# Fourier mixing and tanh shrink on one core: first-stage steps in the third gap alone, output stores issued ahead of the next transposes, other queues and warm-up passes before the main loop

## The chip, the core and the metric

The kernel runs on one core of a Trainium2 chip. The metric is the time of one execution on the device in microseconds (us), as the median of several runs. TensorE is called PE, VectorE DVE, ScalarE ACT, GpSimd POOL and SyncE SP, as in the profile. Everything is computed in float32.

## The reference

```python
X = np.fft.rfft(x, axis=1)                 # x: (8, 3008, 256)
F = (filt_r + 1j * filt_i)[None, :, :]     # (1505, 256) each
y = np.fft.irfft(X * F, n=x.shape[1], axis=1).astype(np.float32)
t = y.reshape(8 * 3008, 256)
h = t @ moe_w_in                           # (256, 2048)
g = h - np.tanh(h)
out = (g @ moe_w_out).astype(np.float32)   # (2048, 256)
```

The two weights come in as float64 and are converted on the chip.

## The kernel before, in words

**The transforms.** The sequence of 3008 is split into 64 times 47. A batch element passes through three stages. The *first* stage (`first`, six steps of a batch) multiplies blocks of x with a matrix f over the 64 and stores the result in the DRAM tensor `ct1`. The *middle* stage (`middle`, seven slots of up to five frequencies, 58 steps of a batch) goes over the 47 forwards (products pa and pb), multiplies with the filter on DVE, goes back (product pe) and stores in `ct2` through a tile e. The *last* stage (`last`, once for each group) makes the tokens of a group: it loads a tile e2 (called e in the profile, too) and a matrix gt, multiplies them (product pu), and forms ut from an ACT copy and two DVE operations. A batch has six groups, so there are 48 groups in all.

**The main loop.** For each group and each quarter u of the 2048 hidden columns there is one unit U, 192 in all. A unit runs the products of w_in (`up`, tiles x, y, z), the shrink function (`shrink`: three activations of 1024 elements for each half, then a DVE product h) of the unit before, and the products of w_out (`down`, tiles o) of the unit before that. Seven products stand for eight through sums of blocks (Strassen's way), which POOL forms (`combine`, tiles t and tu). For the first four units (`up_plain`, `down_plain`) there are eight plain products.

**The order is written out by hand.** What a unit does stands in program order in `up`: x and y products; gap t(0); two down products; gap t(1); x, z; two down products; gap t(2); x; two down products; x; gap t(3); one down product; gap t(4); z. (For groups 0, 6, 12 and so on, t(1) and t(3) stand a little elsewhere.) These five places are the first to the fifth gap. In each gap `t(k)` issues, in this order: the stores of a first-stage step made earlier (list `written`, on ACT), in the third gap the DVE transposes of a finished output tile (`store`, tile ot, which has one buffer), four of the waiting output stores (`store_some`, on SP, 32 or 48 for a group), and one step of the first or middle stage that is due. The list `steps` holds the steps of a batch with their due places, sorted; of the first two, the first that is due and allowed is taken. The third gap of every fourth quarter is kept for `last`. From the fourth unit on a first-stage step may stand in the second and third gap of the first three quarters, unless a step pb stood in the gap before.

**Banks.** A step of the first stage (for batches from 3 on, in quarter form: 64 by 64 tiles of the array, 16 instructions) needs two PSUM banks, tags t and y. The bank y also holds the y product of the unit, until DVE has added it (L549). A middle step takes t, or y in some of the second to fourth gaps.

**Within a unit on ACT**: a copy s of x behind the first x product, a copy u behind each of the next two x products, and between them the activations of `shrink`. The next x product accumulates in the same bank and waits for the copy. A quarter step adds an ACT copy (L285) and two DVE operations (L286, L287), a back step pe an ACT copy (L379) and a store from ACT's queue (L381).

**DMA semaphores.** All DMAs from SP and ACT together take turns on eight completion semaphores, in program order, and those from POOL on eight others. A DMA waits, on the engine that issues it, until the one that had its semaphore before has landed.

**The prologue** handles batch 0 as a whole and part of batch 1 with its own tiles (`first0`, `across`, `back0`), converts the first weights (`early`, then `late`), and loads the tile e of group 0 piece by piece (`rest`, L981: eight loads; 25 rows each of slots 0 to 4, then 7 rows each of slots 5 and 6). Slots 0 to 4 are stored to `ct2` from POOL, slot 5 from ACT, slot 6 half from ACT and half from SP (L381). `warmer(n)` issues n products whose result is not used.

Of the kernel before, what the change touches and what calls it, by code (L numbers as in the profile page):

```python
# [21 lines left out]
SG = 5  # L22
# [4 lines left out]
NC = NH // CH  # L27
NX = NH // XH
SLOTS = [(a, min(SG, NA - a)) for a in range(0, NA, SG)]
KM = SG * NH  # L30
# [67 lines left out]
def kernel(  # L98
# [114 lines left out]
    def begun(tiles, job, queue=nc.sync):  # L213
        j = converted(tiles, *job, queue)
        next(j)
        return j
# [583 lines left out]
    def store_some(n):  # L800
        for dst, src in outs[:n]:
            nc.sync.dma_start(dst, src)  # L802
        del outs[:n]
# [93 lines left out]
    with tc.tile_pool(name="tr", bufs=2) as tr, tc.manual_schedule():  # L897
# [12 lines left out]
        with tc.tile_pool(name="pro", bufs=1) as pro, \  # L910
# [26 lines left out]
            def warmer(n, t=None):  # L937

                warm = z0("warm", [128, 256])
                t = f0[:, 0:2].rearrange("p a n -> p (a n)") if t is None else t  # L940
                for _ in range(n):
                    nc.tensor.matmul(warm, t[:, 0:128], t, start=True, stop=True)
# [34 lines left out]
            def rest(a, n, queues):  # L977

                e2 = e2s[0][0]
                for j in range(4):  # L980
                    queues[j % len(queues)].dma_start(  # L981
                        e2[NA * j + a:NA * j + a + n],
                        dram(ct2[0], (NA * j + a) * NH * DM, [[NH * DM, n], [1, CH * DM]]))

            def back0(g, nn):

                way = ways(g, 1, KM)
                for v in range(2):
                    pe = z0("pe", [128, 2, DM])[0:KM]
                    for k in range(2):  # L990
                        nc.tensor.matmul(pe[:, k], way[2 * v + k], nn[:, k],
                                         start=True, stop=False)
                        nc.tensor.matmul(pe[:, k], way[3 - k if v else 0], nn[:, 2 + k],
                                         start=False, stop=True)
                    e1 = pro.tile([128, 2, DM], F32, tag="e1", bufs=4, name="e1")[0:KM]
                    ACT.copy(e1, pe)
                    (G if g < len(SLOTS) - 2 else ACT).dma_start(
                        next(parts(ct2, 0, g, v, 2, 2))[2], e1)

            pairs = []  # L1000
# [102 lines left out]
            def way_back():  # L1103

                product, what = ended.pop(0)
                for _ in product(*what) or ():
                    pass
# [4 lines left out]
            for g in range(last_g + 1):  # L1112
                if g + 2 <= last_g:
                    fts[g + 2] = filters_of(g + 2)
                    a2[g + 2] = across(g + 2)
                if g == 3:
                    e2s[0] = load_e2(0, 0, ())
                    ones_1 = first1(load_x(big([128, 8, DM], F32, "x1"), 1, 0, 8))
                if g == last_g - 1:
                    under(fts[last_g])  # L1120
                    convert(3)
                    way_back()
                if g < last_g:
                    there[g + 1] = there0(g + 1)
                next(there[g][0])
                if g < last_g - 1:
                    convert(3)
                xy = there.pop(g)[1]
                chain = filtered(g, xy, fts.pop(g), V, V if g >= last_g - 1 else G, pro)
                nn = next(chain)  # L1130
                for _ in range(2):
                    next(chain)
                if g in summed:
                    next(chain)
                ended.append((back, (0, g, xy, z0, (ACT, nc.sync))) if g in summed else (back0, (g, nn)))
                if g not in (0, last_g - 1):
                    way_back()
                if g == 1:
                    next(turning)
                if g == 2:  # L1140
                    ahead = [begun(tiles1, job, queue=G) for job in jobs[5:7]]
            way_back()
            rest(0, SG * (last_g - 1), [nc.sync])
            rest(SG * (last_g - 1), NA - SG * (last_g - 1), [nc.sync])
            fs = first(2, z2, [(1, c) for c in range(2, NX)])
            next(fs)
# [3 lines left out]
            next(late)  # L1150
            for _ in ones_1:
                pass
            warmer(10)

        with tc.tile_pool(name="dn", bufs=2) as dn, \
                tc.tile_pool(name="ps", bufs=1, space=bass.MemoryType.PSUM) as ps:
# [46 lines left out]
            total = 4 * len(groups)  # L1203
            for _ in last(0, z2):
                pass
            for _ in range(4):
                next(late)
            def planned(p):
# [12 lines left out]
            for U in range(total + 2):  # L1221
                i, u = divmod(U, 4)
                if U == 6:
                    assert not pending
                    late = sums(7)
                if U < total:
                    p, c = groups[i]
                    if c == 0 and u == 0:
                        steps = planned(p)
                    if u == 0 and i + 1 < len(groups) and c + 1 < NC:  # L1230
                        e2s[i + 1] = load_e2(*groups[i + 1])
                    if u == 2 and i + 1 < len(groups) and c + 1 == NC:
                        assert not steps
                        e2s[i + 1] = load_e2(*groups[i + 1])
                    if u == 1 and c + 1 == NC:
                        for gens, ahead, what in ((mids, 2, middle), (firsts, 3, first)):
                            if p + ahead < BATCH:
                                gens[p + ahead] = what(p + ahead, z1 if what is middle else z2)
                                next(gens[p + ahead])
                    if u == 2 and i + 1 < len(groups):  # L1240
                        lasts = last(i + 1, z2)
                sh = shrink(U - 1) if 0 <= U - 1 < total else iter(())
                dw = iter(())
                if 0 <= U - 2 < total:
                    dw = (down if U - 2 >= 4 else down_plain)(U - 2)

                def converting(n):

                    for _ in range(n):
                        if next(late, pending) is pending:  # L1250
                            pending.clear()

                def d():

                    next(dw, None)

                def e():

                    next(dw, None)
                    converting(3 if U > 1 else 1)  # L1260

                def s():

                    next(sh, None)

                def t(k):

                    now[:] = U, k
                    if k == 0 and U >= 4:
                        taken.clear()  # L1270
                    while written:
                        ACT.dma_start(*written.pop(0))
                    if k == 2 and stores:
                        store(*stores.pop())
                    store_some(4)
                    if U >= total:
                        return
                    pos = 20 * c + 5 * u + k
                    if i == 1 and pos == LEAD - 7:
                        mids[1] = middle(1, z1)  # L1280
                        next(mids[1])
                    if u == 3 and k == 2 and i + 1 < len(groups):
                        next(lasts)
                    else:
                        due = [s for s in steps[0:2] if s[0] <= pos and
                               (s[3] is middle or U < 4 or
                                u < 3 and 0 < k < 3 and taken.get("slow") != k - 1)]
                        if due:
                            steps.remove(due[0])
                            _, gens, b, what, n = due[0]  # L1290
                            if b not in gens:
                                gens[b] = what(b, z1 if what is middle else z2)
                                next(gens[b])
                            next(gens[b])
                    converting(2)
                    if k and U > 1:
                        next(copies, None)

                if U < total:
                    if U == total - 1:  # L1300
                        ones = cst.tile([128, 1], F32, name="ones")
                        G.memset(ones, 1.0)
                    (up if U >= 4 else up_plain)(U, d, e, s, t)
                else:
                    for k in range(5):
                        s()
                        s()
                        d()
                        if U == total + 1 and k in (0, 2):
                            next(bound)  # L1310
                        e()
                        t(k)
# [39 lines left out]
```

## Time and profile before

| | |
|---|---|
| median of three runs | 2680.51 us (2680.18 to 2681.63) |
| the profiled execution | 2680.11 us, its span 2678.3 us |
| PE busy | 2641.6 us, 99% of the span |
| DVE, ACT, POOL busy | 66%, 63%, 49% |
| mean granted clock of PE | 0.994 |
| DMA | 198.20 MB, 74 GB/s over the span |

The span goes from the first to the last instruction. A row of a timeline reads: start, duration (us), engine, line, operation, out<-in, shapes, number of instructions merged, and in brackets the idle time before it and what ended it. `ACTq` and `SPq` are the queues of ACT and SP, whose DMA issues are not counted as busy. A matrix product in float32 stands as two instructions, and the end of a product overlaps the start of the next, so the pace is read from start to start. The granted clock is 1.00 at full speed and 0.50 at half.

### The profile page before, as it was taken

What the parts mean: (1) busy time and instruction counts of PE and PEld (TensorE: products, weight loads), DVE (VectorE), ACT (ScalarE), POOL (GpSimd) and SP (SyncE); (2) the same over time, 40 slices, a digit from 0 to 9 for tenths busy, and PEclk for the clock granted to TensorE, in tenths of its full rate; (3) what the DMA queues carried; (4) which work ended last, traced back from release to release, by engine and by line L of the source; (5) the groups of instructions that cost most, each with busy time, mean ns of one, the idle gap of its engine ahead of it and who ended that gap; (6) DMA issues with size and microseconds to landing.
All of it is one profiled execution on the core that took longest, in us unless ns stands there. A gap on an engine that the chain in (4) does not pass through costs nothing.

```text
span 2678.3 us, 41269 instructions
## 1 busy us (share of the span) xinstructions
PE 2641.6 (99%) x15460; PEld 2292.6 (86%) x15460; DVE 1780.1 (66%) x2234; ACT 1684.2 (63%) x2517; POOL 1312.4 (49%) x1084
## 2 busy tenths in 40 slices
PE   8899999999999999999999999999999999999998
PEld 7578889888898888988889888898888988898887
DVE  6677766767576675767657776577666776655555
ACT  4465666666666666666666666666666666666665
POOL 4116455544454554555455545455455554555552
PEclk9899999999999999999999999999999999999999
DMA  8753332331334313432234232423322221111110
GB/s 221 229 157 87 80 71 69 92 86 39 72 75 104 72 37 74 101 76 68 53 70 105 65 73 53 99 66 75 73 56 57 51 66 42 29 28 26 22 24 18
DMA packets 341960, 198.20 MB, mean 74 GB/s; under 512 B 240415, under 2 KB 312715, under 8 KB 341687
## 3 DMA queue, kind: packets, MB, share of 16 engines
q1 hardware_dynamic: 300877, 137.21, 22.4%
q10 hardware_dynamic: 36698, 45.63, 6.0%
q0 software_dynamic: 4176, 12.64, 1.6%
q8 instruction: 123, 2.02, 0.3%
q14 instruction: 86, 0.70, 0.1%
HBM read 123.22 MB, written 75.00 MB: 74 GB/s over the span
## 4 chain that ended last, share of the span: by engine, by line
PE 91%; DMA 3%; DVE 2%; issue 1%; ACT 1%; SPq 1%; POOL 0%; ACTq 0%; DVEq 0%; POOLq 0%
PE o L696 40%; PE x L526 24%; PE z L526 12%; PE y L526 6%; PE pe L376 3%; PE pu L485 2%; PE pb L328 2%; PE pa L328 1%; PE pf L280 1%; PE o L750 1%; DMA out_dram<-ot 1%; DMA filt<-in_filt_r_dram 1%; SPq L802 0%; PE pf L268 0%; DMA ct<-a 0%
## 5 line engine op out<-in xcount | busy, mean ns | idle before, releaser
L696 PE MATMUL o<-t,wd 128*128 128x256 f32 (+1 forms) x3008 | 759.7, 375 | 0.0
L648 DVE TENSOR_TENSOR h<-h,y 128x1024 f32<-128x1024 f32 (+1 forms) x384 | 553.3, 1441 | 167.8 <-ACT y L644 167.3
L506 POOL TENSOR_TENSOR t<-h 128x512 f32<-128x512 f32 (+1 forms) x186 | 256.4, 1379 | 819.2 <-DVE h L648 763.6
L696 PEld LDWEIGHTS o<-t,wd 128*128 128x128 f32 x3008 | 570.5, 190 | 67.3
L526 PE MATMUL x<-tu,wu 128*128 128x256 f32 (+1 forms) x2256 | 580.5, 380 | 4.7 <-ACT u L532 4.6
L696 PE MATMUL o<-h,wd 128*128 128x256 f32 (+1 forms) x2256 | 570.0, 375 | 1.8 <-DVE h L648 1.8
L526 PEld LDWEIGHTS x<-tu,wu 128*128 128x128 f32 x2256 | 418.7, 190 | 73.8 <-issue 12.5
L696 PEld LDWEIGHTS o<-h,wd 128*128 128x128 f32 x2256 | 427.6, 190 | 52.5 <-DVE h L648 2.6
L532 ACT COPY s<-x 128x512 f32<-128x512 f32 (+1 forms) x188 | 108.7, 578 | 538.6 <-PE x L526 529.6
L638 ACT ACTIVATE y<-h 128x1024 f32<-128x1024 f32 (+1 forms) x384 | 400.3, 1042 | 16.5 <-ACT e L379 9.6
L641 ACT ACTIVATE y<-y 128x1024 f32<-128x1024 f32 (+1 forms) x384 | 399.3, 1040 | 12.1
L644 ACT ACTIVATE y<-y 128x1024 f32<-128x1024 f32 (+1 forms) x384 | 399.9, 1041 | 5.1 <-ACT a L270 0.4
L532 ACT COPY u<-x 128x512 f32<-128x512 f32 (+1 forms) x376 | 215.1, 572 | 100.5 <-PE x L526 76.6
L507 POOL TENSOR_TENSOR t<-h,t 128x512 f32<-128x512 f32 (+1 forms) x186 | 266.6, 1433 | 14.6
L509 POOL TENSOR_TENSOR t<-h,t 128x512 f32<-128x512 f32 (+1 forms) x186 | 264.3, 1421 | 0.0
L508 POOL TENSOR_TENSOR t<-h 128x512 f32<-128x512 f32 (+1 forms) x186 | 261.0, 1403 | 0.0
L574 DVE COPY h<-x 128x512 f32<-128x512 f32 (+1 forms) x188 | 127.9, 681 | 131.6 <-PE x L526 130.8
L566 DVE TENSOR_TENSOR h<-z,u 128x512 f32<-128x512 f32 (+1 forms) x188 | 126.8, 674 | 99.6 <-ACT u L532 98.3
L526 PE MATMUL x<-ut,wu 128*128 128x256 f32 (+1 forms) x752 | 190.3, 375 | 0.0
L526 PE MATMUL y<-ut,wu 128*128 128x256 f32 (+1 forms) x752 | 190.1, 375 | 0.0
L526 PE MATMUL z<-tu,wu 128*128 128x256 f32 (+1 forms) x752 | 190.0, 375 | 0.0
L526 PE MATMUL z<-ut,wu 128*128 128x256 f32 (+1 forms) x752 | 190.0, 375 | 0.0
(163 smaller groups left out, 2969.2 us busy)
## 6 DMA issues: line engine op xcount, KB each, us to landing
e<-ct SPq DMA_DIRECT2D x47, 512.0 KB
ct<-e ACTq DMA_DIRECT2D x86, 240.0 KB
a<-ct SPq DMA_DIRECT2D x42, 480.0 KB
ft<-filt SPq DMA_DIRECT2D x42, 480.0 KB
out_dram<-ot SPq DMA_DIRECT2D x1248, 16.0 KB
x_sb<-in_x_dram SPq DMA_DIRECT2D x74, 256.0 KB
ct<-a ACTq DMA_DIRECT2D x62, 256.0 KB
gt<-g SPq DMA_DIRECT2D x48, 128.0 KB
```

Of the source, the lines that this page charges most:

```text
L506: by.tensor_sub(t[0], b[0][1], b[0][0])
L507: by.tensor_sub(t[1], b[1][1], t[0])
L508: by.tensor_sub(t[2], b[1][1], b[0][1])
L509: by.tensor_sub(t[3], b[1][0], t[1])
L526: nc.tensor.matmul(bank[:, k], wu[:, q - 1, (2 * u + k) * 128:(2 * u + k + 1) * 128], rhs[q - 1], start=(first and k == 0), stop=True, ski ...
L532: ACT.copy(t, X)
L574: V.tensor_copy(h[:, 2, :, 0:w], X)
L638: ACT.activation(y[k], ht[k], AF.Arctan, scale=TURN)
L641: ACT.activation(y[k], y[k], AF.Tanh, scale=BEND)
L644: ACT.activation(y[k], y[k], AF.Square, scale=SCALE, accum_out=y_sums[:, 2 * U + k // 2:2 * U + k // 2 + 1])
L648: V.tensor_mul(ht[k], ht[k], y[k])
L696: nc.tensor.matmul(product(q), wd[:, q - 1, (2 * u + k) * 128: (2 * u + k + 1) * 128], rhs[q - 1][:, k], start=(u == 0 and k == 0 and q == ...
```

## The change

1. First-stage steps (from unit 4 on) stand in the third gap of the first three quarters alone, and the condition on pb is gone. In the built program five of the six steps of each batch from 3 on move from the second gap to the third, 25 in all; the sixth stood there already. Middle steps around them move by a gap.
2. In a gap the four output stores are issued ahead of the transposes of the next tile, not behind, so a tile's first four stores stand one gap later in the order.
3. The generators of the next `middle` and `first`, with their first loads on SP, are begun in the third quarter of a batch's last group instead of the second; `last` is made where it is used.
4. Slot 5's two stores are issued from POOL, not from ACT.
5. The four loads of rows of slots 0 to 4 are issued on SP ahead of slot 6's way back and its stores.
6. `warmer(14)` for `warmer(10)`, and four more warm-up products behind the products pu of group 0.

```diff
@@ -994,7 +994,7 @@
-                    (G if g < len(SLOTS) - 2 else ACT).dma_start(
+                    G.dma_start(
                         next(parts(ct2, 0, g, v, 2, 2))[2], e1)
@@ -1139,8 +1139,8 @@
+            rest(0, SG * (last_g - 1), [nc.sync])
             way_back()
-            rest(0, SG * (last_g - 1), [nc.sync])
             rest(SG * (last_g - 1), NA - SG * (last_g - 1), [nc.sync])
@@ -1150,7 +1150,7 @@
-            warmer(10)
+            warmer(14)
@@ -1203,6 +1203,9 @@
             for _ in last(0, z2):
                 pass
+            warm = psl([128, 256], "o3")
+            for _ in range(4):
+                nc.tensor.matmul(warm[0:KM], mats[:, 0:KM], mats[:, 0:256], start=True, stop=True)
@@ -1232,13 +1235,11 @@
-                    if u == 1 and c + 1 == NC:
+                    if u == 2 and c + 1 == NC:
                         for gens, ahead, what in ((mids, 2, middle), (firsts, 3, first)):
                             if p + ahead < BATCH:
                                 gens[p + ahead] = what(p + ahead, z1 if what is middle else z2)
                                 next(gens[p + ahead])
-                    if u == 2 and i + 1 < len(groups):
-                        lasts = last(i + 1, z2)
@@ -1270,21 +1271,20 @@
+                    store_some(4)
                     if k == 2 and stores:
                         store(*stores.pop())
-                    store_some(4)
                     if U >= total:
                         return
...
-                    if u == 3 and k == 2 and i + 1 < len(groups):
-                        next(lasts)
+                    if (u, k) == (3, 2) and i + 1 < len(groups):
+                        next(last(i + 1, z2))
                     else:
                         due = [s for s in steps[0:2] if s[0] <= pos and
-                               (s[3] is middle or U < 4 or
-                                u < 3 and 0 < k < 3 and taken.get("slow") != k - 1)]
+                               (s[3] is middle or U < 4 or u < 3 and k == 2)]
```

## The prediction

> **What bounds the kernel now.** I read the page first, then the busy times by stage, then the waits and the timelines of the places where TensorE (PE) stood still. The page, its first lines and the chain that ended last:
>
> ```profile
> span 2678.3 us, 41269 instructions
> PE 91%; DMA 3%; DVE 2%; issue 1%; ACT 1%; SPq 1%; POOL 0%; ACTq 0%; DVEq 0%; POOLq 0%
> ```
>
> The busy times by stage (stretch, its length, then busy time of PE, PEld, DVE, ACT, POOL, the granted PE clock, DMA share, GB/s):
>
> ```profile
> 0.00:200.00 200.00, 179.26 (x866) 133.09 (x866) 138.28 (x243) 102.89 (x165) 51.13 (x69) 0.94 0.72 203
> 200.00:2640.00 2440.00, 2433.90 (x14466) 2135.97 (x14465) 1622.76 (x1964) 1565.61 (x2330) 1254.76 (x1008) 1.00 0.27 64
> 67.97:85.02 17.05, 14.06 (x72) 11.78 (x71) 10.83 (x22) 5.58 (x11) 2.22 (x3) 1.00 0.70 209
> 85.03:95.26 10.23, 5.83 (x69) 3.87 (x70) 4.41 (x8) 1.15 (x2) 0.16 (x1) 0.50 0.89 242
> 129.41:136.22 6.81, 5.99 (x10) 3.26 (x11) 3.68 (x10) 0.76 (x2) 0.72 (x1) 0.50 0.38 115
> ```
>
> PE is the bound, and the change takes no real product away. What can be won is PE's idle time: 20.7 us before 200 us, 6.1 us in the 2440 us of the main loop, and the time that PE runs at half clock (10.23 us after one gap in the prologue, 6.81 us after another). The rest is product time.
>
> **The prologue: loads, queues, warm-up passes.** PE's rows around the start of the main loop, and the ACT and DVE rows between them:
>
> ```profile
> 78.10 4.48 PE L942 MATMUL warm<-f 128*128 128x256 f32 x20
> 87.49 2.49 PE L485 MATMUL pu<-gt,e 64*64 64x64 f32 x64 [4.91 <-DMA x_sb<-in_x_dram]
> 90.06 0.59 ACT L489 COPY odd<-pu 128x512 f32<-128x512 f32 x1 [8.99 <-issue]
> 91.89 3.35 PE L596 MATMUL x<-ut,wu 128*128 128x448 f32 x4 [1.91 <-DVE ut L493]
> 95.04 1.78 PE L596 MATMUL z<-ut,wu 128*128 128x448 f32 x4
> 101.39 1.67 PE L596 MATMUL x<-ut,wu 128*128 128x448 f32 x4
> 102.89 1.67 PE L596 MATMUL z<-ut,wu 128*128 128x448 f32 x4
> 130.24 1.86 PE L750 MATMUL o<-h,wd 128*128 128x448 f32 x2 [3.21 <-DVE wd L179]
> 200.27 1.16 PE L485 MATMUL pu<-gt,e 64*64 64x64 f32 x64
> ```
>
> After ten warm-up passes PE waits 4.91 us for the tile e of group 0 (the releaser is named x_sb, but pu reads only gt and e). Then the clock is 0.50 until 95.26: pu takes 2.49 us instead of 1.16, and the four x rows 3.15 us (91.89 to 95.04) instead of 1.50 (101.39 to 102.89). What holds the tile e, by queue:
>
> ```profile
> 67.14 0.74 POOL L997 DMA_DIRECT2D ct<-e  x1 [2.50 <-ACT e L996]
> 69.81 0.74 POOL L997 DMA_DIRECT2D ct<-e  x1 [1.93 <-ACT xy L331]
> 70.55 0.74 POOL L153 DMA_DIRECT2D raw<-in_moe_w_out_dram  x1
> 72.15 0.60 ACTq L997 DMA_DIRECT2D ct<-e  x1
> 73.83 0.34 ACTq L997 DMA_DIRECT2D ct<-e  x1
> 74.81 1.17 SPq L381 DMA_DIRECT2D ct<-e  x2
> 78.74 0.28 SPq L981 DMA_DIRECT2D e<-ct  x1
> 80.27 1.76 SPq L981 DMA_DIRECT2D e<-ct  x5
> ct<-e POOLq DMA_DIRECT2D x1, 240.0 KB, 3.0
> 74.81 5.14 DMA ct<-e
> ```
>
> The first four loads of e need only slots 0 to 4, whose last stores (POOL, 67.14 and 69.81) land 3.0 us after issue, at 72.8. But they stand behind the two SP stores of slot 6, and the second takes over the semaphore of slot 5's first ACT store (72.15), so it goes out only at 78.74, 6.6 us behind that store.
>
> Changed: (1) the four loads come ahead of the slot 6 stores and no longer follow an ACT store; they go out between 70.1 and about 74. (2) Slot 5's two stores go out on POOL ahead of the raw weight loads, at about 72.2 and 73.9, and by the 3.0 us row land by 77. POOL's two raw loads start 3 to 4 us later; nothing else stands behind them on POOL, and the conversions that use them come behind pu in the order of ACT and DVE. (3) The SP stores of slot 6 keep 74.81, since their copies set it. They land 3.0 us (the POOL row) to 5.1 us (the chain's row) later, at 78 to 80. (4) The last four loads then go out by 79.5 to 81. Before, the last was issued at about 81.7 and PE started 5.75 us later; 3.0 is the other end. So e is there between 82.5 and 86.8. I take 83.5, near the early end, because the four large loads no longer stand in front of them.
>
> (5) Fourteen passes at 0.448 us (4.48 for ten) end at 84.4 instead of 82.6, so pu starts at 84.4 with no gap to speak of and full clock. pu 1.16, the wait of 1.91 for ACT and DVE, then x at 87.5 and z at 89.0 against 95.04: **6.0 us**. The four new passes behind pu take 4 x 0.448 = 1.8 us inside the 1.91 us wait; without that cover they would cost up to 1.8. If e comes at 86.8, the gain is about 1. What lies behind is a chain of relative waits and should move along, and the second gap (3.21 us ahead of 130.24, with the half clock of 129.41) should stay. If it went too, another 3.2 us of idle and half of 6.8 us would go.
>
> [...]
>
> **The main loop: first-stage steps.** The waits of PE between 400 and 2640 us, all of them (engine, line, releaser: us, times, longest):
>
> ```profile
> PE x L526 <- ACT u L532: 4.4, 5, 0.9
> PE pf L280 <- DVE h L549: 1.4, 5, 0.5
> ```
>
> Five of each: once per batch. The second kind, with the DVE rows that cause it:
>
> ```profile
> 858.91 1.76 DVE L366 TENSOR_TENSOR xy<-nn 120x512 f32<-120x512 f32 x1
> 860.47 0.65 PE L280 MATMUL pf<-x_sb,f 64*64 64x256 f32 x4
> 862.34 1.13 PE L526 MATMUL x<-tu,wu 128*128 128x256 f32 x4
> ```
>
> A quarter step in the second gap needs both banks; y is freed by DVE's L549, here queued behind the adds of the step in the first gap (L366 until 860.67). It takes 1.87 us (860.47 to 862.34). Such a step in the third gap already stands in the trace once per batch:
>
> ```profile
> 625.09 1.09 PE L280 MATMUL pf<-x_sb,f 64*64 64x256 f32 x16
> 626.12 1.13 PE L526 MATMUL x<-tu,wu 128*128 128x256 f32 x4
> 627.08 1.89 PE L696 MATMUL o<-t,wd 128*128 128x256 f32 x8
> 627.28 0.59 ACT L532 COPY u<-x 128x512 f32<-128x512 f32 x1 [0.42 <-PE x L526]
> 628.81 1.03 PE L526 MATMUL x<-tu,wu 128*128 128x256 f32 x4
> ```
>
> It takes 1.03 us, and u is copied at 627.87, 0.94 us before PE needs it at 628.81. The change moves 25 steps (five per batch) from the second gap to the third. Five are worth 0.84 each, **4.2 us**; the other 20 cost and win nothing. The middle step that leaves the third gap goes to the second or fourth, where such steps stand already. For the bound above: the copy L285 now stands ahead of the u copy on ACT; if ACT comes an activation (1.06) later than at 627, 0.12 is lost per step, 3 us in all.
>
> **The main loop: stores.** The first kind of wait:
>
> ```profile
> 680.88 3.08 DMA out_dram<-ot
> 682.29 1.89 PE L696 MATMUL o<-t,wd 128*128 128x256 f32 x8
> 684.03 0.35 ACTq L381 DMA_DIRECT2D ct<-e  x1
> 685.06 1.13 PE L526 MATMUL x<-tu,wu 128*128 128x256 f32 x4 [0.88 <-ACT u L532]
> ```
>
> The store of e on ACT takes over the semaphore of the first output store behind the transposes (680.88), waits until it lands, and holds up the u copy behind it on ACT. The same eight products take 1.73 us at 627.08 (to 628.81), so 685.06 is 1.04 late; five times, **5.2 us**. In the changed order the first-stage step stands in this gap, its ct stores and the e store come a gap later, when the output stores ahead have been out longer, and the next u copy stands ahead of them. What is late then is the copy s of the next step: its use has the slack of a gap (0.9) or more. Ends: 0 won (the wait moves to s) and 5.2; I take 5.2, since the same layout at 625 us has no wait. The first loads of the two stages that run ahead start one unit later, two units before their use; a unit is about 13.4 us (192 of them between 91.89 and the tail), so 27 us are left for transfers of 3 to 6: nothing.
>
> **Sum.** 6.0 + 4.2 + 5.2 = 15.4 us off the profiled execution of 2680.11 (span 2678.3 and 1.8 around it): 2664.7. The runs' median is 0.4 above it: **2665**.
>
> **Rivals.** (B) The prologue's gain is given back, since e lands at 86.8 or DVE's weight conversions set the pace before 130 us anyway: 9.4 to 10.4 us are left, 2671. For it: DMA share 0.89 in that stretch; against: the chain is one of waits on each other. (C) The main loop's waits only move (the e store waits for a later output store, the step for the bank of the middle step ahead of it): 6.0 are left, 2674.5. For it: a group's output stores still go out in a row while ACT stores; against: 625 us. (D) Both, so that the change does not do what it says: 2680. (E) Slower: in the third gap ACT is regularly late, its copy L285 ahead of u, and PE waits at the second x product behind it. Price per step: two activations (2.12) less the 0.94 of slack = 1.18, times 25 = 29.5, so 2694. It decides from (15.4 + 5.4) / 25 = 0.83 us per step. Against it: no such wait in five steps of before; for it: a late u copy does reach PE (685.06).
>
> [...] The trace has 0.50 from 129.41, when the stop that ended at 130.24 was 2.4 us old, so a late e of two or three us would cost clock as well.
>
> **How the numbers follow.** Forecast 0.60 (own range 2660 to 2670: the moved copy up, a shorter second gap down), B 0.12, C 0.12, D 0.06, E 0.10. 0.2% is 5.4 us, about what a measurement can tell from no change. Faster 0.84, same 0.06, slower 0.10. The range takes in B and C, and below, the second gap gone: 2658 to 2676.
>
> **What would show it.** Right: PE's idle time before pu under 1 us, no 0.50 clock between 85 and 95 us, z at about 89; 30 quarter steps of 1.03 us behind the second down products, no PE wait on L549; no ACT store waiting ahead of a u copy once per batch. Wrong: waits of x on u or s in every batch, of y L526 on the copy L379, or a clock of 0.50 behind 85 us. The prediction falls if waits of over 0.8 us stand behind most moved steps.

## The result: 2670.7 us against 2680.4, and the profile after

| | before | after |
|---|---|---|
| median of six runs each, on the same chip | 2680.35 us (2680.11 to 2681.63) | 2670.68 us (2669.85 to 2671.94) |
| ratio, 95% interval | | 0.9961 [0.9951, 0.9972] |
| profiled execution: time, span | 2680.11, 2678.3 us | 2670.29, 2668.5 us |
| mean granted clock of PE | 0.994 | 0.997 |

The change makes the kernel 9.7 us faster. The forecast was 15.4 us faster: the right side, inside the range of 2658 to 2676, but 5.7 us short. The page of after, its first line and the chain that ended last:

```profile
span 2668.5 us, 41319 instructions
PE 94%; DVE 2%; DMA 2%; ACT 1%; issue 1%; SPq 0%; ACTq 0%; POOL 0%; DVEq 0%; POOLq 0%
```

The busy times by stage of after (columns as in the prediction):

```profile
0.00:200.00 200.00, 184.30 (x973) 138.74 (x974) 145.02 (x251) 104.98 (x169) 57.70 (x75) 0.98 0.71 202
84.20:91.00 6.80, 6.48 (x80) 4.23 (x81) 4.14 (x8) 1.69 (x3) 0.00 (x0) 1.00 1.04 259
124.30:127.70 3.40, 3.15 (x5) 1.52 (x6) 2.05 (x6) 0.22 (x2) 0.67 (x1) 0.50 0.50 190
213.05:219.85 6.80, 5.79 (x14) 4.57 (x15) 3.98 (x6) 1.63 (x3) 1.63 (x2) 0.50 0.39 122
```

The clock is full where it was 0.50 before (85 to 95 us), and the half-clock stretch at the second gap is 3.4 us long in place of 6.8. But there is a new one of 6.8 us from 213, in a place where before had none.

To see where the time went, cut both traces at points that they share and compare the lengths. The points are the first product L1079, the first z product L596, and the first pu product of groups 1, 2, 3, 4 and 47:

| stretch | before | after | difference |
|---|---|---|---|
| start to L1079 (PE has met no edit yet) | 74.65 | 73.22 | -1.43 |
| L1079 to z | 20.39 | 16.29 | -4.10 |
| z to group 1 | 45.34 | 43.77 | -1.57 |
| group 1 to 2 | 59.89 | 58.16 | -1.73 |
| group 2 to 3 | 56.04 | 64.53 | +8.49 |
| group 3 to 4 | 57.16 | 57.16 | 0.00 |
| group 4 to 47 | 2285.82 | 2275.04 | -10.78 |
| group 47 to the end | 79.05 | 80.35 | +1.30 |

The eight add up to -9.82 us, the difference of the spans. The first is put down to chance: L1079 came at 73.9 to 75.0 us in the profiles of the four programs with the old queues, and at 73.2 to 76.4 in the ten with the new. In the last, the way from the product L814 to the end is 1.3 us longer. That is hardly chance: it takes 11.8 to 12.4 us in all eight profiles of the changed kernel and of those made from it below, and 10.7 to 11.2 in the six of the kernel before and of those made from that. What causes it stays open. The -1.73 is a step of L268 (a row of x8) that moved from the stretch behind group 1 into the next, so the two stretches together have lost 6.8 us.

**The prologue.** PE's rows of after that answer to 78.10 to 95.04 and 130.24 of before:

```profile
76.67 6.21 PE L942 MATMUL warm<-f 128*128 128x256 f32 x28
84.19 0.33 PE L485 MATMUL pu<-gt,e 64*64 64x64 f32 x4 [1.31 <-DMA e<-ct]
84.84 1.15 PE L485 MATMUL pu<-gt,e 64*64 64x64 f32 x60 [0.32 <-issue]
85.92 1.99 PE L1208 MATMUL pt<-mats_sb 120*120 120x256 f32 x8
87.90 1.77 PE L596 MATMUL x<-ut,wu 128*128 128x448 f32 x4
89.50 1.67 PE L596 MATMUL z<-ut,wu 128*128 128x448 f32 x4
124.55 1.86 PE L750 MATMUL o<-h,wd 128*128 128x448 f32 x2 [3.17 <-DVE wd L179]
```

The wait for e is 1.31 us in place of 4.91. The four passes (L1208) fill the time in which ACT and DVE make ut, x runs at full speed, and the stop ahead of the second gap stays. The queues behind it:

```profile
69.05 3.87 SPq L981 DMA_DIRECT2D e<-ct  x4
70.98 0.74 POOL L997 DMA_DIRECT2D ct<-e  x1 [1.86 <-ACT e L996]
72.71 0.74 POOL L997 DMA_DIRECT2D ct<-e  x1 [0.98 <-ACT e L996]
73.38 1.16 SPq L381 DMA_DIRECT2D ct<-e  x2
78.22 2.70 SPq L981 DMA_DIRECT2D e<-ct  x4
```

Counted from L1079 (74.65 before, 73.22 here), the issue times are about those of the prediction, up to the last four loads: the forecast has them out by 6.4 us behind L1079 at the latest (81), and the last goes out 7.4 behind it (80.63), before 7.1 (81.74). The landings are not those forecast: slot 5's two POOL stores took 3.5 and 5.1 us, slot 6's stores 4.6 to 5.6, and the last four loads 4.1 to 5.4 (the last 4.1, before 6.0); the tile was complete at 84.75, before at 87.77.

**The main loop.** All of PE's waits from 140 to 2600 us:

```profile
PE x L526 <- ACT u L532: 4.2, 2, 4.0
```

Both waits that came once per batch are gone; from 400 us on none is left. From its first to the next instruction, each of the 30 quarter steps now takes 1.02 us; before, 25 did, and five took 1.87 to 2.14. The one large wait stands in unit 8:

```profile
205.21 0.38 SPq L307 DMA_DIRECT2D a<-ct  x1
205.69 0.42 SPq L315 DMA_DIRECT2D ft<-filt  x1
207.03 1.83 SPq L802 DMA_DIRECT2D out_dram<-ot  x4
207.51 0.58 ACT L270 COPY a<-pf 128x512 f32<-128x512 f32 x1 [0.28 <-PE pf L268]
208.17 1.89 PE L696 MATMUL o<-t,wd 128*128 128x256 f32 x8
213.05 0.33 ACTq L273 DMA_DIRECT2D ct<-a  x1
213.42 0.58 ACT L532 COPY u<-x 128x512 f32<-128x512 f32 x1 [5.33 <-DMA out_dram<-ot]
214.06 2.08 PE L526 MATMUL x<-tu,wu 128*128 128x256 f32 x4 [4.00 <-ACT u L532]
```

This is the last step of batch 2 (`first`, L268), which is a whole step, not a quarter step. Its store L273 is issued from ACT in the same gap, not put on the list `written`. By the turn of the eight semaphores it takes over that of the third output store of the row 207.03. That one was issued at 207.97 and landed at 212.98, 0.07 us before the store went out; the loads a (480 KB, landed after 5.1 us) and ft (480 KB, 6.8 us, at 212.46) were under way ahead of it. ACT stood until then with the u copy queued behind the store; PE stood for 4.0 us and then ran at half clock for 6.8. Before, this step stood in the third gap of unit 6, with the step ahead of it in the second gap. By the new rule that one takes the third gap of unit 6, the third gap of unit 7 is kept for `last`, and so this step waits for that of unit 8.

### The profile page after: what moved, and what is told of

Read it like the earlier page. It is cut to its first block, busy times and chain, and to the rows that moved or that the text cites. A ratio compares the mean times of both kernels' runs of the same rounds, so it can differ in the third digit from the quotient of the medians.

```text
span 2668.5 us, 41319 instructions
## 1 busy us (share of the span) xinstructions
PE 2637.3 (99%) x15476; PEld 2297.0 (86%) x15476; DVE 1790.7 (67%) x2234; ACT 1682.0 (63%) x2517; POOL 1324.7 (50%) x1086
## 4 chain that ended last, share of the span: by engine, by line
PE 94%; DVE 2%; DMA 2%; ACT 1%; issue 1%; SPq 0%; ACTq 0%; POOL 0%; DVEq 0%; POOLq 0%
PE o L696 41%; PE x L526 24%; PE z L526 12%; PE y L526 6%; PE pe L376 3%; PE pu L485 2%; PE pb L328 2%; PE pa L328 2%; PE pf L280 1%; PE o L750 1%; PE pf L268 0%; DMA fh<-f 0%; DMA e<-ct 0%; SPq L802 0%; DMA out_dram<-ot 0%
## 5 line engine op out<-in xcount | busy, mean ns | idle before, releaser
L526 PE MATMUL x<-tu,wu 128*128 128x256 f32 (+1 forms) x2256 | 581.1, 380 | 4.2 <-ACT u L532 4.2
L526 PEld LDWEIGHTS x<-tu,wu 128*128 128x128 f32 x2256 | 420.5, 190 | 70.0 <-ACT u L532 9.0
L532 ACT COPY s<-x 128x512 f32<-128x512 f32 (+1 forms) x188 | 108.6, 578 | 539.2 <-PE x L526 517.8
L532 ACT COPY u<-x 128x512 f32<-128x512 f32 (+1 forms) x376 | 214.4, 570 | 80.7 <-PE x L526 65.0
L526 PE MATMUL x<-ut,wu 128*128 128x256 f32 (+1 forms) x752 | 190.4, 376 | 0.0
L526 PE MATMUL z<-ut,wu 128*128 128x256 f32 (+1 forms) x752 | 190.4, 376 | 0.0
L526 PE MATMUL y<-ut,wu 128*128 128x256 f32 (+1 forms) x752 | 190.2, 376 | 0.0
L526 PE MATMUL z<-tu,wu 128*128 128x256 f32 (+1 forms) x752 | 190.1, 375 | 0.0
L549 DVE TENSOR_TENSOR h<-y,s 128x512 f32<-128x512 f32 (+1 forms) x188 | 126.9, 675 | 78.0 <-PE y L526 59.3
```

Of the source, the lines that this page charges most:

```text
L526: nc.tensor.matmul(bank[:, k], wu[:, q - 1, (2 * u + k) * 128:(2 * u + k + 1) * 128], rhs[q - 1], start=(first and k == 0), stop=True, ski ...
L532: ACT.copy(t, X)
```

## The experiments

Two things had to be settled: which edit took the two waits of each batch away (the prediction credits the moved steps with one and the store order with the other), and what the new stall is. Then what the parts of the prologue are worth. The experiments form three series, each with the kernel before beside it, which took 2681.7, 2681.6 and 2681.8 us as a median (2677.9 to 2687.6 over all its runs); ratios are to that of the same series.

**Batch 2 in the old gaps.** The changed kernel, with steps of batches up to 2 allowed in the second gap again.

```diff
-  (s[3] is middle or U < 4 or u < 3 and k == 2)]
+  (s[3] is middle or U < 4 or
+   u < 3 and (k == 2 or k == 1 and s[2] <= 2 and taken.get("slow") != 0))]
```

> The changed kernel, but first-stage steps of batch 2 (whole form, stored straight from ACT) may stand in the second or third gap as before. Theory A: the new wait of PE near 210 us and the half clock behind it (6.8 us together) come from the last batch-2 step, which the new rule moved to unit 8; without the move about 2664 us, no PE wait over 1 us between 140 and 2600 us. Theory B: the exchange of stores and transposes alone makes ACT's store wait there; then about 2670.5 us, and a wait of some 4 us stays between 140 and 260 us.

Measured: 2666.22 us (2664.68 to 2668.4), ratio 0.9937 [0.992, 0.9953]. Its waits of PE from 140 to 2600 us:

```profile
PE x L526 <- ACT s L532: 1.3, 1, 1.3
PE x L526 <- ACT u L532: 0.2, 1, 0.2
```

The stall is gone, and group 2 to 3 takes 56.10 us, as before (56.04). So the 6.8 us belong to the places of the batch-2 steps (the last series pins them to the store of the last one), and the gain from group 4 on (2276.25 against 2285.82) does not depend on them. The wait on the copy s, at 1598 us, is another matter: one or two such waits of 1.25 to 1.40 us stand in five of the fourteen profiles, with the old rule too (the queues alone, the passes alone), and none over 0.3 in the others.

**The old store order.** The changed kernel, with `store_some(4)` behind the transposes again.

```diff
-                    store_some(4)
                     if k == 2 and stores:
                         store(*stores.pop())
+                    store_some(4)
```

> The changed kernel with the output stores behind the transposes again. Theory A: all moved steps stay, so both kinds of once-per-batch wait stay away; the ct store of unit 8 now takes over the semaphore of the load a<-ct in place of that of an output store, which landed 2.6 us earlier in the changed kernel, so the wait there falls from 4.2 to about 1.6 us and the clock may stay whole: 2665 to 2668 us. Theory B (and the prediction's working): the wait of x on u once per batch comes back, 5 x 1.0, on top of whatever is left at 210 us: 2671 us or more.

Measured: 2667.73 us (2664.48 to 2668.95), 0.9941 [0.9924, 0.9957]. The waits of each batch stay away. Unit 8:

```profile
212.07 0.33 ACTq L273 DMA_DIRECT2D ct<-a  x1
212.44 0.59 ACT L532 COPY u<-x 128x512 f32<-128x512 f32 x1 [4.18 <-DMA a<-ct]
213.08 1.98 PE L526 MATMUL x<-tu,wu 128*128 128x256 f32 x4 [2.85 <-ACT u L532]
```

The store now follows the load a (landed at 212.00) in place of an output store. The stall is 1.15 us shorter (the expectation had 1.6 us left of it, 2.85 are), and half clock lasts 3.4 us. The new store order therefore wins nothing here and costs 1.1 to 2.3 us at this place (group 2 to 3 takes 62.23 us, against 63.34 to 64.54 in the three profiles that have the stall and the new order).

**The moved steps alone**, in the kernel before (the new rule is the only edit):

```diff
-  u < 3 and 0 < k < 3 and taken.get("slow") != k - 1)]
+  u < 3 and k == 2)]
```

> The kernel before with the third-gap rule alone. Theory A: 5 x 0.85 and 5 x 1.1 go, about 10 us, less some 2 to 5 us for a wait at unit 8: 2672 to 2675 us. Theory B: 5 x 0.85 goes, the waits of x on u stay: about 2676 us, or more with a wait at unit 8.

Measured: 2672.5 us (2671.94 to 2674.92), 0.9966 [0.9953, 0.9978]. Waits from 140 to 2600 us:

```profile
PE x L526 <- ACT u L532: 2.5, 2, 2.3
PE x L526 <- ACT s L532: 1.4, 1, 1.4
```

Both kinds of once-per-batch wait are gone without any other part. Group 4 to 47 takes 2276.77 us, 9.05 less than before. The stall at unit 8 (2.3) is there too: it comes with the new rule. The unit that has the wait at 685.06 in before looks like this with the new rule alone:

```profile
679.65 1.09 PE L280 MATMUL pf<-x_sb,f 64*64 64x256 f32 x16
681.84 0.59 ACT L532 COPY u<-x 128x512 f32<-128x512 f32 x1 [0.44 <-PE x L526]
684.23 1.03 PE L376 MATMUL pe<-xy,mats_sb 120*120 120x256 f32 x4
687.32 0.35 ACTq L381 DMA_DIRECT2D ct<-e  x1
687.89 0.59 ACT L532 COPY s<-x 128x512 f32<-128x512 f32 x1 [2.00 <-PE x L526]
```

The step L280 has the third gap and pe the fourth. The store of e (687.32) stands behind the u copy, ahead of a copy s that was waiting for PE anyway.

**The store order alone**, in the kernel before (the reverse of the second experiment's edit).

> The kernel before with the output stores ahead of the transposes alone. Theory A: nothing that counts, the e store of unit 42 still takes over the semaphore of the first output store of a tile: 2680 to 2681 us, five waits of x on u left. Theory B: these five waits are gone: about 2675 us.

Measured: 2679.25 us (2677.3 to 2683.85), 0.9991 [0.9981, 1.0001]. Its waits:

```profile
PE x L526 <- ACT u L532: 4.9, 7, 0.9
PE pf L280 <- DVE h L549: 1.7, 5, 0.6
```

Both kinds of wait stay as before. With the run above, this settles which edit did it: the step that moved into the third gap pushes the back step pe, and so the store of e on ACT, out of the place ahead of the u copy.

**The queues alone**, in the kernel before (parts 4 and 5, ten passes), **the passes alone** (part 6), and **the queues with 14 passes** but without the four behind pu.

```diff
-  (G if g < len(SLOTS) - 2 else ACT).dma_start(
+  G.dma_start(
...
+  rest(0, SG * (last_g - 1), [nc.sync])
   way_back()
-  rest(0, SG * (last_g - 1), [nc.sync])
```

> The kernel before with slot 5's stores on POOL and the four early loads of e ahead of slot 6's stores, ten warm-up passes. Theory A (from the four profiles so far): the queues bring e about 1 us earlier against the first first-stage product (some 11.3 instead of 12.3 us behind it), PE still waits some 3.5 us and the half clock stays: 1 to 1.5 us under the kernel before. Theory B (the prediction's working): e is there 3 to 4 us earlier, at most 9 us behind that product: 4 us or more under it.

> The kernel before with 14 passes and the four passes behind pu, queues as before. Theory A: e is as late as before, PE waits some 2.7 us ahead of pu, but the stretch at half clock is shorter or gone, which is most of the prologue's gain: 2 to 3.5 us under the kernel before. Theory B: the passes only fill a wait; without an earlier e under 1 us.

> The kernel before with the queues and 14 passes, without the four passes behind pu. Theory A: the stop of 2 us behind pu, in one window with the wait ahead of it, brings back a stretch at half clock in some executions: 2.5 us under the kernel before, against about 3.5 with the four passes. [...]

Measured: 2681.86 us (0.9999 [0.9989, 1.0009]), 2677.37 us (0.9982 [0.9972, 0.9991]) and 2679.54 us (0.9997 [0.9987, 1.0006]). Theory A of the three had 1 to 1.5, 2 to 3.5 and 2.5 us under the kernel before; it came to nothing, 4.3 and 2.1, and only the passes alone stand clear of no change. The totals tell little, because the kernels with the old rule differ in the main loop between executions: group 4 to 47 took 2284.65 to 2290.41 us in these three profiles and 2285.82 before. So read the prologue by itself, from L1079 to the landing of e and from there to z:

| program | L1079 to e landed | e landed to z |
|---|---|---|
| old queues, 10 passes (before, and the two runs above) | 13.12, 11.64, 12.22 | 7.27, 7.27, 7.27 |
| new queues, 10 passes | 10.72 | 7.12 |
| old queues, 14 and 4 passes | 11.93 | 4.91 |
| new queues, 14 passes | 11.06 | 6.30 |
| new queues, 14 and 4 passes (after, six of the kernels here) | 10.63 to 11.66, mean 11.30 | 4.75 or 4.76; once 6.18 |

The queues bring e 1.0 us earlier (means of 12.23 over four programs without them, 11.21 over the nine of this table with them). The 14 passes win 0.8 to 1.0 us from there to z, the four behind pu another 1.55; this rests on one execution without the four. The 6.18 is one with them, in which the half clock fell on the four passes themselves: they took 3.41 us up to x in place of 1.98. Rows of PE in the kernel with the queues and 14 passes, then its busy time over the stretch of half clock (PE alone, then clock, DMA share, GB/s):

```profile
77.77 6.21 PE L942 MATMUL warm<-f 128*128 128x256 f32 x28
85.00 1.61 PE L485 MATMUL pu<-gt,e 64*64 64x64 f32 x64 [1.02 <-DMA e<-ct]
88.52 3.35 PE L596 MATMUL x<-ut,wu 128*128 128x448 f32 x4 [1.91 <-DVE ut L493]
91.67 1.77 PE L596 MATMUL z<-ut,wu 128*128 128x448 f32 x4
```

```profile
88.40:91.80 3.40, 3.28 (x5) 0.51 1.05 280
```

Behind two stops of 1.02 and 1.91 us came 3.4 us at half clock: x took 3.15 us to z, as before. With the four passes in the second stop it takes 1.60.

**Still more passes**: the first experiment's kernel with `warmer(18)`.

```diff
-            warmer(14)
+            warmer(18)
```

> The changed kernel, batch-2 steps placed as before and 18 warm-up passes instead of 14. They end some 11.5 us behind the first first-stage product, about when e lands. Theory A: no wait ahead of pu and no half clock behind it, 1 to 2 us under the kernel with batch 2 as before and 14 passes: about 2664 us. Theory B: e lands by itself when it does, the clock stays half in a window that the wait does not touch: the same 2666 us, or up to 0.8 us more where e was there earlier.

Measured: 2666.03 us (2665.74 to 2668.19), 0.9943 [0.9926, 0.9959]; the same with 14. The passes ended at 87.37 and e had landed at 87.51, so there was no wait left, but z came 4.76 us behind e, as in six of the seven profiles with 14: there the passes only replaced a stop (1.31 us in after) that no half clock followed. The profile of the first experiment itself is the seventh, with the 6.18 above.

**The store of that step, one gap later; from POOL; the loads begun earlier; and the changed kernel again** (the third series). The first puts the one store on the list `written`, the second has `G.dma_start` in that branch. The third undoes part 3 (`u == 1` for `u == 2`).

```diff
-  ACT.dma_start(dram(ct1[b], ...), a1...)
+  way = (dram(ct1[b], ...), a1...)
+  if b == 2 and k == len(jobs) - 1:
+      written.append(way)
+  else:
+      ACT.dma_start(*way)
```

> The changed kernel, with the ct store of the last first-stage step of batch 2 put on the list that is drained a gap later, as the quarter steps' stores are, in place of at once on ACT. Theory A (the store, waiting on ACT for a transfer still in flight, holds up the u copy behind it, and that is the whole 4.2 us stall and the 6.8 us at half clock behind it): the step itself stays in the third gap of unit 8, the wait of PE on u there falls from 4.0 to under 1.0 us, no half clock behind 213 us, the way from group 2 to group 3 shortens from 64.5 to about 58, and the time is 6 to 7 us below the changed kernel's of the same call: 2664. Rival B (the stall is the step's own, since eight large products and two bank copies stand in that gap beside the filter's and the weights' loads): the stall stays at 2.5 us or more and the time at 2668 or above. Rival C (the wait only moves on to copy s of the next unit): under 2 us are won, 2669.

> The changed kernel, with the ct store of the last first-stage step of batch 2 issued from POOL in place of ACT. Theory A: POOL's semaphores are others and its queue holds no store for SP's outputs, so ACT goes straight to the u copy: the stall at unit 8 falls under 1.0 us, group 2 to group 3 takes about 58 us, 2664. Rival B (the stall is the step's own): 2.5 us or more stay there, 2668 or above. Rival C: POOL, which waits there for the two bank copies of ACT before it can issue, is late with the sums tu, and PE waits for these in place of u: 1 to 3 us of the gain are lost, 2666.

> The changed kernel with part 3 alone undone: the next middle and first stages and their first loads are begun in the second quarter of a batch's last group again. Both the prediction and theory A say that this is worth nothing: within 1 us of the changed kernel in the same call, the stall at unit 8 as it was (4 us, half clock behind it), main-loop waits otherwise none. Rival: the loads, one unit later, stand ahead of the output stores in SP's queue and change which transfer the late ACT stores take over from; then the once-per-batch waits come back, up to 5 x 1.04 = 5 us slower, or the stall at unit 8 changes by 2 us or more.

> The changed kernel unaltered, for its time and its spread beside the other three of this call. Every theory: 2669.5 to 2672; a stall of about 4 us at unit 8 (3.5 to 4.6 if it is a wait for a landing that varies little), and a start of the main loop that moves by one to two us between executions.

| | median us (range) | ratio to before, 95% | group 2 to 3 |
|---|---|---|---|
| store one gap later | **2663.66** (2661.34 to 2665.56) | 0.9932 [0.9918, 0.9945] | 57.43 |
| store from POOL | 2665.27 (2663.42 to 2667.72) | 0.9937 [0.9923, 0.995] | 57.43 |
| loads begun earlier | 2673.39 (2669.98 to 2678.3) | 0.9974 [0.9963, 0.9985] | 63.34 |
| changed kernel again | 2671.03 (2669.41 to 2671.61) | 0.9959 [0.9945, 0.9972] | 64.54 |

Theory A holds: the step stays in its gap, with its products (the row of x8) and two copies, and the stall goes. Unit 8 of the kernel with the store one gap later (its lines from L277 on are four further down, so L536 is the copy L532, L530 the product L526):

```profile
206.82 1.89 PE L268 MATMUL pf<-x_sb,f 128*128 128x256 f32 x8
209.61 0.59 ACT L536 COPY u<-x 128x512 f32<-128x512 f32 x1 [0.28 <-PE x L530]
211.14 1.03 PE L530 MATMUL x<-tu,wu 128*128 128x256 f32 x4
214.64 0.33 ACTq L1277 DMA_DIRECT2D ct<-a  x1
215.66 0.59 ACT L536 COPY s<-x 128x512 f32<-128x512 f32 x1 [4.41 <-PE x L530]
```

The store still goes out only at 214.64, later than in the changed kernel. But what stands behind it now is the copy s, which could not start before the x product at 215.46 anyway (4.41 us idle, released by PE). A wait of the same kind costs 7.4 us in one place (2671.03 less 2663.66) and nothing in another. This version is the fastest of all: 18.1 us below the kernel before beside it. From POOL the store goes out at 211.80, and no sum tu came late.

Part 3 is not settled: without it the median is 2.4 us above the changed kernel's, where the expectation had 1 at most, but the runs overlap, and the profiled span is 1.1 us shorter (2668.2 against 2669.3).

## Why the prediction was right, and where it was wrong

The direction came out, and two of the three terms (moved steps and stores). The measured 2670.7 is nearest to rival B's 2671 and just above the forecast's own 2660 to 2670, but B's reason (the prologue's gain is given back) is not what happened: from L1079 to group 1 the profile won 5.7 us and from group 4 on 10.8, where 6.0 and 9.4 were forecast, and a loss that the prediction did not have took 6.8 us of it. A start 1.4 us earlier and an end 1.3 us longer, neither of them forecast, cancel. That the wider range held the time is owed to the room that it gave to B and C.

- **Moved steps, 4.2 us: right.** 25 steps stand in the third gap, all 30 take 1.02 us, and the five waits on L549 are gone. The five long steps of before take 9.71 us together, so 9.71 - 5 x 1.02 = 4.6 were won. The bound for a late ACT (3 us) and rival E (slower, 2694) did not show at a single quarter step.
- **Stores, 5.2 us: right in size, wrong in cause.** The waits on u went: in before the five second x products come 1.03 to 1.10 us late (forecast 1.04), 5.3 in all, and in after none does. With the 4.6 above that makes 9.9 of the 10.78 us won from group 4 on; the other 0.9 is not assigned. But "in the changed order" credits the edit of the stores together with the step; the rule alone took them away, and the store order alone left them all.
- **The step that failed: "The change moves 25 steps".** The prediction went through the quarter steps of batches 3 to 7 and "the other 20 cost and win nothing". The rule also holds for batch 2 and moves three of its steps: two by a gap (units 5 and 6), at no cost that the trace shows, and the last across two units. That one is a whole step whose store is issued at once from ACT, and it comes into a gap behind two 480 KB loads. It lost 6.8 us against before, and 7.1 against the version with its store a gap later (64.53 and 57.43 from group 2 to 3): a stop of 4.0 and close to half of the 6.8 at half clock. The mechanism is the one that the prediction had found in before (an ACT store that takes over the semaphore of an output store, with the u copy behind it), at a place it did not look at. Rival C names the mechanism with the wrong place; no rival had this one. With the store moved out of the way, the kernel takes 2663.7 us, 1.3 from the forecast of 2665.
- **The prologue, 6.0 us: too much, and made of other parts.** z came at 89.50 (forecast 89.0), but 1.43 us of that is an earlier start. From L1079 on, z came 3.3 us earlier by the means of the table's first and last programs (16.26 against 19.60), and group 1 another 1.2 (43.70 behind z against 44.91). The forecast had e at 83.5 and thus 4.3 us earlier. The queues gave 1.0. The 3.0 us landing of a POOL store held at 67 and 70 us in before, but the page of before has 4.8 as the median of its ten, and in after the stores of slot 5 took 3.5 and 5.1 us, with loads of e and of weights under way beside them. Slot 6's stores took up to 5.6 us, and so the last loads went out 1 us later than forecast at the latest. The landing of before (13.12 us behind L1079) was also late for that program; two other executions had 11.64 and 12.22. The larger part came from the passes, by keeping the clock (1.00 from 84.20 to 91.00). PE's idle time ahead of pu, forecast under 1 us, is 1.31 and 0.32.
- **The four passes cost nothing**, inside the 1.91 us, and won 1.55 us: in the one execution without them (the queues and 14 passes), half clock followed the stops of 1.02 and 1.91 us, and PE was busy for 1.45 of the 3.41 us ahead of it.
- **The second gap stayed**, as forecast: its stop is 3.17 us. Its half clock is 3.4 us in after and in both kernels above with the old prologue and one edit of the main loop, 6.8 in before; so that difference is chance of the execution, not the change's. Over eight profiles (before, after, the first two experiments and the four of the prologue) stops of 2.97 to 3.62 us there were followed by half clock of 6.8 us three times (before, the passes alone, the queues with 14 passes), of 3.4 us four times and of none once (the old store order).

## What to carry to other kernels

When a scheduling rule changes, list every step that it moves, the odd ones of the start too, and for each the DMA it issues and what stands behind that issue on the same engine. In this kernel a store issued from ACT stood until the transfer that held its completion semaphore had landed (213.05 in after, 0.07 us behind a landing at 212.98; 684.03 in before, 0.07 behind one at 683.96); put it where the next instruction of that engine is waiting for something else anyway. And judge a prologue from a point ahead of the edits over several executions, since here its landings alone moved by 1.0 to 1.5 us between executions. In before and after, half clock followed the full-clock steps of 3.41 us in which PE was busy for at most 1.57 us, and none with 1.99 or more (below), so filling even a short stop can pay: the four passes won 1.55 us.

## What the runs showed of the hardware

A transfer went out behind the landing of the one ahead of it on its semaphore. In before and in after, this holds for each of the 2296 transfers that have one ahead; the shortest time between the two is 0.02 us, and in 99 and 95 cases it is under 0.15.

Small stores landed at different times behind different loads. In after, the output stores (12 and 4 KB) issued at 207.0 to 208.4, when the loads of 480 KB of 205.21 and 205.69 were under way, landed between 212.63 and 213.15, 0.17 to 0.18 us apart and in the order of issue, 4.7 to 5.6 us after issue; those issued at 212.5 to 212.9 (12 KB), when both loads had landed, took 1.4 to 1.5. What sets the order of the landings was not shown.

Half clock came in steps of 3.41 us: stretches of 3.41 (62.83 in after), 6.83 (129.40 in before) and 10.24 us (85.03 in before). A stop of 4.0 us (unit 8) was followed by 6.83 us of it, one of 2.85 us (the old store order) by 3.4. Stops of 1.31 us (after) and 2.16 us (the passes alone) ahead of pu were followed by none, while one of 1.39 us (batch 2 in the old gaps) was followed by 3.41. So here a stop's length alone did not tell.

The busy share of a step told more. In before and after the stretches of half clock begin whole steps of 3.413 us apart: in before at 61.13, 85.03 and 129.40 (7 and 13 steps), in after at 62.83, 124.27 and 213.02 (18 and 26). Cut these two traces into such steps and count PE's busy time in each one that ran at full clock. The eight that were followed by half clock have at most 1.57 us of it (57.72 in before), the 1540 that were followed by full clock at least 1.99 (2658.68 in before). Two steps, with PE's busy time, then clock, DMA share, GB/s; the first is the queues with 14 passes, with half clock behind it, the second is after, with none:

```profile
85.03:88.44 3.41, 1.45 (x64) 1.00 1.01 258
83.31:86.72 3.41, 2.21 (x68) 1.00 0.99 230
```

How a stop falls on the steps thus went with what it cost. In the same two traces the steps at half clock that were followed by another one have 0.92 to 2.58 us of busy time, those that were followed by full clock 3.14 to 3.42. The stop of unit 8 leaves 2.37 us in its first step at half clock (213.02), and a second follows; the second gap of after leaves 3.14 (124.27), and none follows.
